# A fused attention and feed-forward kernel: a new order of steps for all five engines

## The chip, the cores and the metric

The kernel runs on one core of one Trainium2 chip. A core has five engines that each take their instructions strictly in turn: TensorE (PE: matrix products, with its weight loads shown apart as PEld), VectorE (DVE), ScalarE (ACT), GpSimd (POOL) and SyncE (SP), which here only starts DMA transfers; ACT and POOL start some as well. The metric is the time of one execution on the device in microseconds; lower is better.

## What is computed

Sparse attention over 4 batches x 8 heads x 768 positions x 64 dimensions, then a feed-forward net (FFN) over the 3072 tokens x 512 features that come out. The reference, cut to what matters:

```python
k_min = np.min(k_chunks, axis=3)            # chunks of 32 keys, 24 per head
k_max = np.max(k_chunks, axis=3)
ub = np.sum(np.maximum(q[:, :, :, None, :] * k_min[:, :, None, :, :],
                       q[:, :, :, None, :] * k_max[:, :, None, :, :]), axis=-1)
ub = np.where(causal, ub, -1000000000.0)
top_chunks = np.argsort(ub, axis=-1)[..., -top_k:]       # the best 6 chunks of each query
scores = scale * np.matmul(q, k.transpose(0, 1, 3, 2))
mask = sel & (pos[:, None] >= pos[None, :])
attn = softmax(np.where(mask, scores, -1000000000.0))
x = np.matmul(attn, v)                      # heads side by side: 3072 x 512
xn = x / np.sqrt(np.mean(x * x, -1) + 1e-06) * rms_g
g = xn @ w_gate                             # 512 x 1536
out = (g / (1.0 + np.exp(-g)) * (xn @ w_val)) @ w_out
```

## The kernel before

The work is cut into twelve blocks of 256 query positions. `ORDER` (L340) lists them as (batch, third of the sequence): block 0 is (0,0), block 4 is (0,1), block 5 is (1,1), block 6 is (0,2), block 8 is (1,2). Each block has two groups of four heads, g = 0 and 1.

**Attention of a block.** k and q arrive by DMA (`load k...`, `load q...`, L376, started by SP, a few by ACT; v by POOL). DVE turns them (`turn k`, `turn q`, L636), takes minimum and maximum of each chunk (`ext0`, `ext1`, L651) and their difference (`dk`, L657). Copies in bf16 (`half k`, `half q`, L643 on ACT or L644 on POOL) feed the scores. For the bounds, q is copied into QX (`qx`, L691/L692) and, from block 4 on, four small transfers per block started by SP bring the other halves across partitions (`qm0` to `qm3`, L706); `relu` (L731 on ACT, L733 on POOL or DVE) needs all four. TensorE makes the bounds (`upper`, L522, or L540 for the first blocks), DVE picks the six best chunks (`ubn`, `top`, `mk`, `mt`, `swap`), TensorE makes the scores (`scores`, L760, with the mask added at L771), ACT the exponentials (`exp`, L810), POOL cuts the triangle (`tri`, L780), TensorE multiplies by v (`values`, L836), and DVE divides (`rden`, `norm`, L851 and L855).

**Between the two.** ACT sums squares (`square`, L872), POOL makes the root (`rms`, L878 and L880), and the tokens are scaled. For blocks 0 to 3 TensorE turns them (`turn`, L916); from block 4 on DVE scales (`scale`, L890) and SP starts two transposing DMAs per block, one for each 128 tokens (`across40` and `across41` for block 4, L896), into the tile xsT.

**FFN of a block.** Twelve slices of the hidden layer, two at a time, named by the first: `wg(4, (0, 1)).2` is the gate product of block 4, both token halves, slices 2 and 3 (L960); `wv` the value product (L960 too); ACT takes tanh (L967) and copies the value product for POOL (`vcopy`, L979); DVE makes `tg` (L971); the product `hh` is made by POOL (L982) or DVE (L975). `project4.0` multiplies the slices 0 to 9 of the first 128 tokens by w_out (L1008), and `project4.0+` the last two; `out` (L1023 on ACT, L1026 on DVE) and `store` (L1030, SP) finish.

**Weights and fillers.** w_gate, w_val and w_out come in thirds, started by POOL (`wg0` and so on) in between its other work. While weights and first blocks are on their way, TensorE multiplies the identity (`keep_busy`, L1075): the warm-up products.

**What sets the order.** All steps (1550) are first registered with `plan.op` as `Op` objects, each with its engine, or with several that could do it, its inputs, and the buffers that it takes. Nothing is emitted then. `Plan.run` (L227) walks a tuple of whole numbers, `STEPS` (L47), and emits one step for each: the number divided by 8 is the step, the rest the engine (0 PE, 1 ACT, 2 DVE, 3 POOL, 4 SP). So 5628 is step 703, `load q1210` (a q load of block (1,2)), on SP. A negative number stands for a run of warm-up products. `SLOTS` (L156) says which buffer of its pool each step takes. The order of the emission is the order on each engine; semaphores for data and for buffers are added by the framework.

```python
        for x in self.STEPS:
            if x < 0:
                n, slot = divmod(-x, 16)
                fill[-1](n // 2, slot, n % 2)
                continue
            seq, e = divmod(x, 8)
            o = self.ops[seq]
            o.alts[self.ENGINES[e]][2]()
```

Of the kernel before, what the change touches and what calls it, by code (L numbers as in the profile page):

```python
# [33 lines left out]
class Plan:  # L34
# [13 lines left out]
        27, 228, 233, 249, 244, 131, 123, 34, 155, 3, 99, 257, 276, 83, 203, 281, 67, 268, 107, 291,  # L48
        75, 115, 412, 425, 299, 433, 420, 538, 139, 466, 380, 396, 473, 482, 490, 404, 545, 42, 498,
        388, 522, 506, 515, 179, 594, 529, 611, 315, -688, 616, 562, 601, 672, 554, 626, 571, 681,  # L50
        50, 578, 457, 786, 587, 634, 323, -178, 792, 642, 689, 57, 848, 650, 802, 699, 810, 9, 818,
        857, 443, 658, 865, 665, 826, 875, 834, -208, 704, 1098, 841, -48, 736, 912, 713, 746, 1107,
        922, 754, 721, 930, 1185, 1042, -146, 880, 307, 961, 1114, 889, 19, 731, 1058, 897, 971,
        -146, 760, 1066, 1049, 770, 1075, 778, 977, 1082, 1091, 1170, 907, -211, 1248, 1192, 1257,
        1660, 451, 1130, 1177, 984, 1628, 1138, 936, 195, 1644, 1202, 1265, 1147, 1684, 1121, 1362,
        1210, 1154, 1163, 946, 1275, 1676, -112, 1368, 954, 1668, 1218, 331, 1001, 994, 1424, 1312,
        1636, 1433, 1226, 8384, 1378, 1652, 1011, 1234, 1441, 1322, 1242, 8344, 1386, 1330, 147,
        1451, 1017, 1394, 1402, 1280, 339, 1410, 8369, 1024, 1418, 1289, 1488, 347, 8336, 1498,
        1297, 1034, 355, 8401, 1506, 1456, 8353, 8480, 8410, 1307, 1537, 8362, 363, 1336, 8497,
        8488, 1346, 1547, 1762, 1473, 8528, 8506, 1465, 1851, 8513, 1354, 1483, 1778, 8545, 8379,  # L60
        8536, 1553, 1706, 1512, 371, 8561, 8392, 1522, 1530, 8523, 1834, 1560, 1577, 8432, 1570,
        8417, 1587, 8554, 8696, 8449, 1722, 8571, 8688, 8458, 8721, 1730, 1593, 8584, 8705, 1802,
        1739, 171, 2001, 1747, 1600, 8714, 1755, 8576, 8609, 1610, 1841, 8731, 1856, 8440, 1713,
        2212, 1866, 8427, 1794, 2228, 8736, 8593, 1874, 2260, 1811, 8465, 1771, 2268, 8602, 8784,
        2276, 1882, 2244, 1890, 8792, 1818, 1827, 1898, 8475, 8801, 1906, 8753, 8832, 8817, 1699,
        8762, 1912, 2220, 8810, 8849, 8619, 2008, 2308, 1921, 2236, 8744, 2018, 2252, 1691, 1937,
        2026, 2034, 8624, 8769, 2042, 8858, 1931, 1785, 2050, 8779, 2284, 2057, 2354, 2324, 8888,
        2292, 3050, 2363, 2300, 2064, 1947, 2370, 8632, 2347, 2316, 2073, 2378, 8656, 2332, 2089,
        2083, 2868, 2426, 2804, 2387, 8913, 2099, 2820, 8641, 2450, 8827, 1952, 2844, 2104, 2442,
        8664, 2828, 8880, 1962, 2410, 8673, 2459, 2395, 2852, 2403, 2114, 1976, 1970, 2417, 2900,  # L70
        2122, 8840, 8897, 2836, 2482, 2884, 8928, 1986, 8906, 8865, 2466, 2475, 2499, 3611, 2507,
        2128, 1994, 8923, 8945, 2138, 2512, 2146, 2153, 2924, 8875, 2161, 2916, 8936, 2860, 2522,
        8954, 3476, 2171, 8976, 2530, 2812, 2538, 2946, 8684, 2177, 3508, 2546, 8961, 2186, 2908,
        2554, 8971, 2962, 2561, 2192, 2892, 2986, 9008, 2433, 2876, 2339, 2201, 3484, 3010, 3524,
        2491, 3034, 3532, 3019, 2970, 3540, 2568, 3003, 3492, 8984, 3066, 2577, 4148, 9136, 8994,
        3083, 2593, 3026, 9040, 2587, 9153, 2603, 3516, 2656, 9162, 9057, 3116, 2979, 3043, 9048,
        2953, 4283, 9066, 3500, 2665, 3058, 9004, 9096, 3075, 9073, 4212, 2675, 9088, 3618, 2681,
        3108, 163, 9083, 9121, 4252, 3634, 9144, 9105, 3092, 3642, 2691, 9240, 3100, 9114, 9169,
        3588, 2608, 9131, 9016, 9265, 2618, 3556, 2626, 2696, 9025, 2632, 2706, 4164, 2714, 2720,
        9179, 4236, 9184, 2730, 2745, 2642, 3572, 2650, 2738, 3131, 9232, 4220, 9201, 3682, 3123,  # L80
        4228, 2753, 9192, 9210, 4180, 211, 9249, 3706, 4244, 2763, 3136, 9217, 9258, 2777, 9227,
        9280, 3146, 2769, 3596, 3625, 9275, 5596, 9288, 3154, 3658, 2993, 3564, 3162, 2784, 3580,
        3675, 9313, 9328, 3548, 3691, 2793, 4196, 3722, 2931, 4260, 4172, 9297, 3170, 4204, 9400,
        9306, 4268, 3178, 9496, 4860, 9323, 9425, 9036, 3738, 3185, 9392, 4156, 3698, 3651, 3755,
        4188, 9336, 4290, 9409, 3603, 3764, 3192, 4330, 9521, 3780, 9488, 3747, 9418, 3201, 3772,
        3715, 4402, 9435, 9440, 9345, 3788, 4306, 3217, 9360, 4876, 3730, 4347, 4417, 4339, 9457,
        4354, 3667, 9505, 9466, 8652, 3211, 3232, 4378, 4452, 2939, 9514, 4884, 9536, 3241, 5532,
        4314, 3227, 4444, 9448, 3803, 9553, 4428, 3249, 3795, 9562, 9544, 4868, 4370, 9473, 3304,
        1620, 9569, 4386, 4322, 3808, 4436, 4394, 3313, 9579, 4916, 3329, 9592, 4908, 3818, 9483,
        4892, 4297, 9368, 4924, 3826, 9617, 3834, 3344, 3323, 4940, 9377, 4980, 3339, 3256, 3353,  # L90
        4972, 3842, 3280, 4900, 9584, 4459, 3290, 3361, 4932, 3266, 3850, 9531, 9632, 3274, 9601,
        3298, 3857, 3368, 9610, 5548, 3392, 3378, 9649, 4956, 9627, 9640, 3386, 3402, 4964, 3417,
        3410, 3864, 5580, 9658, 4275, 3425, 5644, 9680, 5002, 3873, 9356, 4363, 5106, 4948, 3889,
        3435, 5564, 5066, 9665, 9388, 3458, 3904, 4465, 3442, 9675, 9712, 3913, 5018, 3883, 3452,
        5026, 3899, 3921, 5090, 3468, 5042, 3976, 5082, 4472, 5059, 3985, 5628, 5122, 5035, 4411,
        5612, 4001, 9688, 4482, 3995, 9720, 9697, 5139, 4016, 4490, 4498, 5049, 4011, 5148, 3928,
        9729, 5172, 3952, 4025, 3938, 5098, 9792, 5156, 3962, 4506, 4033, 5164, 9840, 3970, 3946,
        9809, 4514, 4040, 9865, 9800, 9818, 4521, 5604, 4050, 5714, 9832, 6308, 6356, 5114, 4592,
        9849, 5620, 5179, 4058, 6332, 4064, 4601, 9826, 5572, 5187, 9928, 4074, 5588, 9858, 5011,
        4089, 5652, 9880, 4082, 187, 5075, 4609, 5636, 5723, 5192, 5540, 4097, 6340, 9953, 6324,  # L100
        4528, 4107, 5202, 9897, 5556, 9920, 4537, 9906, 4114, 9752, 9937, 4130, 4547, 4553, 4124,
        9968, 5730, 9777, 9946, 4563, 4568, 9985, 5786, 9875, 5129, 9976, 5674, 4577, 91, 4140,
        9994, 9888, 5803, 4585, 6426, 4995, 9744, 9914, 6316, 6364, 4616, 10002, 9761, 6348, 5738,
        4640, 6244, 4626, 9770, 6292, 4664, 6260, 6442, 10072, 4673, 5690, 5812, 4634, 10256, 6284,
        4689, 4683, 5210, 5218, 6276, 5747, 10089, 10080, 9740, 10281, 219, 9963, 5820, 4650, 4704,
        10098, 6268, 4658, 4987, 10120, 6980, 4713, 7628, 5226, 10208, 10105, 7020, 5754, 5795,
        10137, 10160, 4721, 9787, 10146, 10168, 6506, 6300, 6252, 5698, 4728, 6521, 7036, 5234,
        10177, 5707, 10008, 5683, 5828, 10193, 5762, 10115, 6540, 5241, 6386, 7644, 10186, 10225,
        7028, 4737, 6402, 10248, 10203, 5836, 6450, 6548, 10128, 4745, 10234, 6371, 7676, 6410,
        10016, 6988, 5771, 10296, 6490, 4699, 9708, 10025, 6916, 10265, 5248, 10154, 7636, 10313,  # L110
        4776, 10274, 6532, 5257, 6466, 6556, 4752, 5273, 5267, 6474, 6996, 10304, 5843, 4762, 6948,
        4770, 5667, 5288, 10322, 6956, 10036, 4786, 10216, 5778, 5659, 5297, 7652, 4794, 10040,
        5851, 4801, 10330, 6419, 4809, 5283, 10242, 7660, 5305, 6483, 7004, 6435, 6498, 7012, 4819,
        5856, 6457, 10291, 5360, 5866, 7692, 10048, 7724, 5369, 4826, 5312, 6932, 5336, 5385, 6940,
        5379, 10336, 6964, 5346, 5322, 10057, 5874, 5395, 5330, 7684, 6569, 5882, 4836, 5400, 6562,
        4842, 6576, 5409, 5354, 4852, 5890, 10368, 5417, 5898, 7732, 6586, 6513, 6924, 7098, 5906,
        10344, 7115, 5424, 7708, 10354, 5448, 7740, 5912, 5434, 5458, 10068, 7058, 10376, 7748,
        5921, 5442, 7067, 10496, 6594, 10364, 6602, 7107, 5937, 7716, 10584, 6395, 6972, 10521,
# [988 lines left out]
```

## Time and profile before

| | us |
|---|---|
| median of the 3 runs shown | 291.81 |
| lowest, highest | 290.79, 293.36 |
| the profiled execution | 289.74 |
| span of its trace | 287.9 |

Costliest groups, from the page (line, engine, tiles, count, busy us, mean ns of one):

| group | busy us | mean ns |
|---|---|---|
| L810 ACT exponentials, x104 | 85.7 | 860 |
| L960 PE gate products, x640 | 72.4 | 262 |
| L960 PE value products, x640 | 71.7 | 262 |
| L1008 PE output products, x272 | 65.7 | 370 |
| L982 POOL hh, x48 | 55.5 | 1165 |
| L971 DVE tg, x72 | 48.3 | 678 |

How the profile is read: it comes from one execution. Busy time is given per engine; the span is cut into 40 slices of 7.2 us, each digit a busy share in tenths. A table of stages gives, for each stretch, its length and then the busy time of PE, PEld, DVE, ACT and POOL, the granted clock of TensorE, the mean number of busy DMA engines' shares summed over the stretch, and GB/s. A row of a timeline gives start, length, engine, line, operation, tiles and count, with idle time ahead of it and what ended that in brackets; rows of SPq and ACTq are DMA issues on those engines' queues. Matmuls are pipelined, so two rows can overlap.

### The profile page before, as it was taken

The numbers are of one execution on the slowest core, as the hardware profiler recorded it, in microseconds if no ns is written. First come the engines' busy times: TensorE is split into PE (matmuls) and PEld (weight loads), VectorE is DVE, ScalarE is ACT, GpSimd is POOL, SyncE is SP. The second block draws the span as 40 slices with busy tenths as digits, with TensorE's granted clock in tenths as the row PEclk, the third lists the DMA queues.
The fourth block names the chain that finished last, engine by engine and source line by source line (L and its number), as shares of the span: only waits on it lengthen the run. The fifth ranks groups of instructions, "written<-read, shape, count | busy, mean of one in ns | idle before, by whom it ended". The sixth has DMA issues, their size and how long they took to land.

```text
span 287.9 us, 11300 instructions
## 1 busy us (share of the span) xinstructions
PE 278.4 (97%) x4642; PEld 209.9 (73%) x4670; DVE 216.8 (75%) x626; ACT 207.5 (72%) x356; POOL 166.9 (58%) x267
## 2 busy tenths in 40 slices
PE   8999899999999999999999999999999999999995
PEld 2559796758777857887764886788678967588763
DVE  3998879798899899799989899987564725274341
ACT  2998787778879988967865696877679766564421
POOL 6789888979888774757682384528125316112420
PEclk9999999999999999999999999999999999999999
DMA  8999999998499594488794514913012500412022
GB/s 179 202 204 217 206 212 146 138 145 164 101 164 165 126 184 79 108 130 154 133 180 86 148 27 95 127 7 75 2 53 61 40 2 1 112 21 56 1 93 89
DMA packets 86387, 31.93 MB, mean 111 GB/s; under 512 B 74816, under 2 KB 81728, under 8 KB 86336
## 3 DMA queue, kind: packets, MB, share of 16 engines
q1 hardware_dynamic: 55616, 22.56, 33.5%
q0 software_dynamic: 29712, 7.87, 27.5%
q10 hardware_dynamic: 1008, 0.79, 1.3%
q8 instruction: 36, 0.59, 0.9%
q14 instruction: 15, 0.12, 0.1%
HBM read 28.58 MB, written 6.29 MB: 121 GB/s over the span
## 4 chain that ended last, share of the span: by engine, by line
PE 78%; DMA 6%; DVE 4%; SPq 4%; issue 2%; ACT 2%; POOL 2%; ACTq 0%; DVEq 0%; POOLq 0%
PE F L960 37%; PE F L1008 20%; PE S L760 7%; PE F L836 6%; DMA wg<-in_moe_w_gate_dram 3%; PE S L771 3%; PE F L522 3%; SPq L706 2%; SPq L376 2%; DMA kraw<-in_k_dram 1%; DMA QX<-qT 1%; DVE kx L651 1%; PE F L540 1%; PE F L1075 1%; DVE kT L636 1%
## 5 line engine op out<-in xcount | busy, mean ns | idle before, releaser
L810 ACT ACTIVATE pt<-S 128x1024 bf16<-128x1024 f32 (+3 forms) x104 | 85.7, 860 | 28.6 <-PE S L771 25.2
L982 POOL TENSOR_TENSOR hh<-tg,vs 128x512 bf16<-128x512 bf16 x48 | 55.5, 1165 | 43.6 <-DVE tg L971 27.2
L960 PE MATMUL F<-xsT,wg 128*128 128x256 bf16 (+1 forms) x640 | 72.4, 262 | 1.2 <-issue 1.1
L960 PE MATMUL F<-xsT,wv 128*128 128x256 bf16 (+1 forms) x640 | 71.7, 262 | 0.2
L1008 PE MATMUL F<-wo,hh 128*128 128x512 bf16 (+1 forms) x272 | 65.7, 370 | 2.1 <-issue 0.9
L971 DVE SCALAR_TENSOR_TENSOR tg<-th,F 128x512 bf16<-128x512 bf16 x72 | 48.3, 678 | 24.9 <-ACT th L967 20.0
L960 PEld LDWEIGHTS <-wg 128*128 128x128 bf16 x640 | 56.0, 98 | 10.1 <-issue 1.6
L960 PEld LDWEIGHTS <-wv 128*128 128x128 bf16 x640 | 56.0, 98 | 8.3 <-issue 0.8
L967 ACT ACTIVATE th<-F 128x512 bf16<-128x512 f32 x72 | 43.0, 605 | 12.5 <-PE F L960 11.6
L780 POOL TENSOR_SCALAR_AFFINE_SELECT pt<-pt 128x512 bf16<-128x512 bf16 x48 | 31.7, 666 | 26.3 <-ACT pt L810 26.2
L1008 PEld LDWEIGHTS <-hh 128*128 128x128 bf16 x300 | 27.5, 98 | 25.8 <-issue 1.2
L979 ACT ACTIVATE vs<-F 128x512 bf16<-128x512 f32 x48 | 28.5, 599 | 9.2 <-PE F L960 6.4
L760 PE MATMUL S<-qb,kb 32*128 32x256 bf16 (+1 forms) x800 | 32.7, 253 | 0.3
L651 DVE TENSOR_REDUCE kx<-kT 128x16 f32<-128x512 f32 x48 | 31.1, 669 | 0.2
L836 PEld LDWEIGHTS <-pt 128*128 128x128 bf16 x672 | 25.4, 98 | 3.7 <-issue 0.2
L836 PE MATMUL F<-VX,pt 128*128 128x65 bf16 x672 | 27.4, 194 | 0.2
L975 DVE TENSOR_TENSOR hh<-tg,F 128x512 bf16<-128x512 bf16 x24 | 16.1, 679 | 10.2 <-PE F L960 10.0
L760 PEld LDWEIGHTS <-kb 32*128 32x128 bf16 x800 | 13.8, 92 | 13.1 <-issue 11.6
L376 POOL DMA_DIRECT2D VX<-in_v_dram x24 | 22.8, 949 | 0.0
L771 PE MATMUL S<-mtd,chunkrow 32*128 32x128 bf16 (+2 forms) x384 | 20.3, 203 | 0.0
L855 DVE TENSOR_TENSOR xnat<-F,rden 128x256 bf16<-128x256 f32 x48 | 19.5, 415 | 0.8
L636 DVE STREAM_TRANSPOSE kT<-kraw 128x512 f32<-128x512 f32 x24 | 16.4, 694 | 4.7 <-DMA kraw<-in_k_dram 4.1
(73 smaller groups left out, 336.8 us busy)
## 6 DMA issues: line engine op xcount, KB each, us to landing
out_dram<-osb SPq DMA_DIRECT2D x23, 256.0 KB, 2.8
kraw<-in_k_dram SPq DMA_DIRECT2D x72, 64.0 KB, 3.3
qraw<-in_q_dram SPq DMA_DIRECT2D x72, 64.0 KB, 2.9
VX<-in_v_dram POOLq DMA_DIRECT2D x24, 128.0 KB, 4.9
QX<-qT SPq DMA_DIRECT2D x32, 64.0 KB, 2.8
wv<-in_moe_w_val_dram POOLq DMA_DIRECT2D x3, 512.0 KB, 9.0
wg<-in_moe_w_gate_dram POOLq DMA_DIRECT2D x3, 512.0 KB, 7.8
wo<-in_moe_w_out_dram POOLq DMA_DIRECT2D x3, 512.0 KB, 13.1
```

The costliest lines, as they stand in the source:

```text
L376: o.inst = issuer[eng].dma_start(out=dst(), in_=src)
L651: plan.op(f"ext{n}{J}", "DVE", 0.585, 0.67, lambda n=n, op=op: VE.tensor_reduce(out=at(kx)[:, g, n], in_=at(kT).rearrange("p h (j c x) -> ...
L760: TE.matmul(s[a // 2][:, a % 2, c0:c0 + q1 - q0], kbt[r, t, ks], qbt[r, t, q0:q1], start=(t == 0), stop=(t == 1 and not mask), skip_group_ ...
L771: TE.matmul(o, chunkrow[r, BLK * kg + P * e:BLK * kg + P * (e + 1)], mv, start=False, stop=(d == 1), skip_group_check=True)
L780: GE.affine_select(out=d, in_=d, compare_op=ALU.is_ge, fill=0.0, base=0, pattern=[[0, 4], [1, P]], channel_multiplier=-1)
L810: lambda pt=pt, hs=hs, c0=c0, c1=c1, x=sc[hp]: SE.activation(out=at(pt)[:, hs, c0:c1], in_=at(x)[:, :, c0:c1], func=ACT.Exp, scale=SCALE), ...
L836: TE.matmul(o[:, a, :], p_[:, a, off:off + P], vt[:, e, 4 * g + a, :], start=(kb_ == 0 and a == 0), stop=(kb_ == nkb - 1 and a == 3), skip ...
L960: TE.matmul(at(p_)[:, n * W:(n + 1) * W], w[:, g, ht * P:(ht + 1) * P], at(xT)[:, g, x0:x0 + W], start=(g == 0), stop=(g == NP - 1), skip_ ...
L967: plan.op(f"tanh{U}.{hp}", "ACT", 0.48, 0.6, lambda th=th, gp=gp: SE.activation(out=at(th), in_=at(gp), func=ACT.Tanh, scale=0.5), pri - 0 ...
L971: VE.scalar_tensor_tensor(out=at(tg), in0=at(th), scalar=1.0, in1=at(gp), op0=ALU.add, op1=ALU.mult), pri - 30, reads=[th, gp], writes=[tg ...
L982: plan.op(f"hh{U}.{hp}", "POOL", 1.11, 1.16, lambda tg=tg, vs=vs, hh=hh: GE.tensor_tensor(out=at(hh), in0=at(tg), in1=at(vs), op=ALU.mult) ...
L1008: TE.matmul(at(op)[:, cs], at(key)[:, o:o + P], wo[:, ht, cs], start=(ht == 0), stop=(ht == NHT - 1), skip_group_check=True)
```

## The change

`STEPS` and `SLOTS` are replaced; nothing else in the file differs. The same 1550 steps are taken.

- TensorE: 315 steps on both sides, 100 of them at another place, by at most six places. The eight runs of warm-up products go from 21, 5, 6, 1, 4, 4, 6, 3 to 21, 4, 1, 3, 4, 2, 6, 2: 43 instead of 50.
- 36 steps change their engine. In the first block: `half k(0,0,0)` from ACT to POOL; `dk(0,0,0)`, two `bd0` (L676) and `relu(0,0,1)` from DVE to POOL; one more `bd0` in block 1; one load from ACT to SP. Later mostly `half`, `qx` and `relu` between ACT, POOL and DVE; at the end `out10.0` and `out10.1` from ACT to DVE.
- ACT: `table`, the tiny exponential at L390 that loads the table (step 1, code 9), stands third on ACT, ahead of two q loads of block 0; before it stood fifteenth.
- POOL: several memsets of the start stand later; the weight loads keep their sequence.
- SP: of 236 steps 181 stand at another place, by up to 34. `load q1210` (5628) goes from behind the transposes of block 4 to ahead of the copies `qm` of block 5, and `load q1220` (5612) to ahead of those transposes (`across40` 3452, `across41` 3468). Five loads of block (3,1) (6244, 6348, 6364, 6316, 6260) go ahead of `across50` and `across51` (4124, 4140). Ahead of `qm1(0,2)` (4436) stand now also `load k2131`, `load k2130`, `load q2100` (4916, 4908, 4924) and 5628; `load k2121` (4884) stands behind it.

The diff, cut to its first lines and to some that hold these codes:

```diff
     STEPS = (
-        27, 228, 233, 249, 244, 131, 123, 34, 155, 3, 99, 257, 276, 83, 203, 281, 67, 268, 107, 291,
...
-        1620, 9569, 4386, 4322, 3808, 4436, 4394, 3313, 9579, 4916, 3329, 9592, 4908, 3818, 9483,
...
-        5026, 3899, 3921, 5090, 3468, 5042, 3976, 5082, 4472, 5059, 3985, 5628, 5122, 5035, 4411,
...
+        27, 228, 233, 249, 244, 115, 50, 67, 34, 131, 3, 99, 9, 257, 276, 123, 268, 107, 281, 291,
...
+        4156, 9336, 4290, 9409, 3192, 5628, 3715, 3755, 9418, 9488, 3201, 4330, 9435, 9521, 9440,
...
+        4297, 4436, 9368, 3826, 9617, 3834, 4892, 3344, 3323, 9377, 4884, 3339, 3256, 4900, 3353,
...
+        3452, 5026, 3921, 5090, 3899, 3468, 5042, 3883, 3976, 5122, 4411, 4472, 3985, 5604, 5082,
...
+        6244, 5179, 5114, 6348, 4592, 9849, 5636, 5723, 4064, 4058, 5540, 5187, 4601, 9826, 5556,
...
     SLOTS = (
-        0, 0, 1, 0, 1, 1, 0, 0, 1, 0, 0, 0, 0, 1, 1, 0, 1, 0, 0, 1, 2, 3, 0, 0, 1, 0, 1, 0, 0, 0, 1,
...
+        0, 0, 1, 1, 0, 1, 0, 0, 1, 0, 0, 0, 1, 0, 1, 0, 1, 0, 1, 0, 0, 0, 1, 2, 3, 1, 0, 0, 0, 0, 0,
...
```

268 rows, old and new, of tables (SLOTS, STEPS) are left out of this document.

## The prediction

> **What bounds the kernel now.** I read the page first (busy times, slices, chain), then the table of stages, then the timelines of the queues around the places where the order changes.
>
> ```profile
> span 287.9 us, 11300 instructions
> ...
> PE 278.4 (97%) x4642; PEld 209.9 (73%) x4670; DVE 216.8 (75%) x626; ACT 207.5 (72%) x356; POOL 166.9 (58%) x267
> ...
> PE   8999899999999999999999999999999999999995
> ...
> PEclk9999999999999999999999999999999999999999
> DMA  8999999998499594488794514913012500412022
> ...
> PE 78%; DMA 6%; DVE 4%; SPq 4%; issue 2%; ACT 2%; POOL 2%; ACTq 0%; DVEq 0%; POOLq 0%
> ```
>
> TensorE is busy 97% of the span and holds 78% of the chain that ended last. It does the same products before and after, bar seven warm-up ones, so only its idle time can go, and a reordering can add idle time without limit. The stages (in each row: length, then each engine's busy time) say where the idle time is:
>
> ```profile
> 0.00:12.00 12.00, 10.47 (x106) 4.65 (x106) 7.01 (x21) 6.64 (x9) 7.60 (x27) 1.00 1.07 185
> 12.00:24.00 12.00, 11.30 (x239) 7.13 (x238) 11.12 (x46) 11.08 (x26) 10.93 (x23) 1.00 1.43 203
> 24.00:36.00 12.00, 10.78 (x241) 10.02 (x239) 10.20 (x23) 9.56 (x20) 10.24 (x15) 1.00 1.21 217
> ...
> 264.00:288.00 24.00, 20.41 (x151) 14.69 (x151) 7.64 (x12) 7.50 (x14) 5.72 (x5) 0.98 0.16 56
> sum 288.00, PE 278.38 PEld 209.88 DVE 216.80 ACT 207.54 POOL 166.92; mean PE 16.38 PEld 12.35 DVE 12.75 ACT 12.21 POOL 9.82
> ```
>
> Idle in all: 288.0 - 278.38 = 9.6 us, of which 1.53 + 0.70 + 1.22 before 36 us and 3.59 in the last stage. The 228 us between hold only 2.6 us. So three places count: the start, the hand-overs in the dense middle, and the end.
>
> **The start (to 36 us).** Here most steps move: the load of the activation table goes ahead of two of ACT's q loads, six small steps go from DVE or ACT to POOL, memsets go behind them, and seven warm-up products go. The weight loads stay in the same sequence.
>
> ```profile
> 30.23 0.32 PEld L960 LDWEIGHTS <-wg 128*128 128x128 bf16 x5 [1.21 <-issue]
> ...
> 33.10 0.90 PEld L960 LDWEIGHTS <-wg 128*128 128x128 bf16 x16 [0.27 <-DMA wg<-in_moe_w_gate_dram]
> ...
> 35.99 0.90 PEld L960 LDWEIGHTS <-wv 128*128 128x128 bf16 x16 [0.21 <-DMA wv<-in_moe_w_val_dram]
> ```
>
> At 33.10 and 35.99 TensorE waits for weights to land, and the DMA row of the page is at eight or nine tenths for its first ten slices (72 us): the weight stream, not the attention of the first block, sets when the dense part begins. Nothing that the change does alters its bytes or its sequence. Attention that is up to 1.21 + 0.27 + 0.21 = 1.7 us late is hidden there; with that cover gone, each us late would be a us lost. The moved table:
>
> ```profile
> 1.74 3.56 ACTq L376 DMA_DIRECT2D qraw<-in_q_dram  x4
> 5.33 1.28 ACT L643 ACT_TABLE_LOAD   x1 [5.33 <-DMA kraw<-in_k_dram]
> ...
> 7.99 0.71 DVE L636 STREAM_TRANSPOSE qT<-qraw 128x512 f32<-128x512 f32 x1
> ```
>
> It costs 1.28 us and sits ahead of the two loads, which then go out at 1.74 + 1.28 = 3.0; DVE wants q only at 7.99, behind four k steps. The six steps given to POOL fit into what it has free in the first stage, 12 - 7.60 = 4.4 us; in the second it has 12 - 10.93 = 1.1. I take 0 for the whole start; the bounds are -1.7 (all three waits go) and +1.1 (POOL's work slips by what it has free in the second stage, and nothing hides it).
>
> **Warm-up products.** They run where TensorE has nothing else to do, so seven fewer save nothing by themselves.
>
> ```profile
> 1.42 7.63 PE L1075 MATMUL F<-ident 128*128 128x512 bf16 x21 [1.42 <-POOL ident masks.py:199]
> ...
> 10.12 1.25 PE L1075 MATMUL F<-ident 128*128 128x512 bf16 x5
> ...
> 12.13 1.47 PE L1075 MATMUL F<-ident 128*128 128x512 bf16 x6
> ```
>
> From five to six they grow by 0.22 us, yet the first 21 took 0.36 us each: an engine that has just started is slow, though the clock column says 1.00. The first 21 stay. The Trainium skill (TensorE: Matmul & The Clock Gate, Part 1: The HAM clock gate) says that an idle window of about 3.4 us halves the matmul clock again. The 21 slow products agree with a slow start; by that rule thinner fillers could mean a second slow spell, which is a rival below.
>
> **The middle: SP's queue.** From 84 us on SP issues without a pause, so a step pulled forward there makes all behind it late. After the change two q loads of block (1,2) (codes 5628, 5612) stand ahead of the two transposes `across4` (L896) that make block 4's FFN input, and five loads stand ahead of `across5`.
>
> ```profile
> 84.03 2.51 SPq L706 DMA_DIRECT2D QX<-qT  x4
> ...
> 93.08 0.59 SPq L706 DMA_DIRECT2D QX<-qT  x1
> 93.72 3.14 SPq L376 DMA_DIRECT2D kraw<-in_k_dram  x3
> 96.97 1.86 SPq L376 DMA_DIRECT2D qraw<-in_q_dram  x4
> ...
> 105.56 2.68 SPq L896 DMA_TRANSPOSE xsT<-xs  x2
> 108.29 1.48 SPq L376 DMA_DIRECT2D qraw<-in_q_dram  x2
> ...
> 121.87 2.54 SPq L896 DMA_TRANSPOSE xsT<-xs  x2
> 124.47 1.67 SPq L376 DMA_DIRECT2D qraw<-in_q_dram  x3
> 126.19 1.44 SPq L376 DMA_DIRECT2D kraw<-in_k_dram  x3
> ```
>
> ```profile
> DMA to landing us min/median/max: 2.4/3.0/4.5
> ```
>
> ```profile
> 100.85 2.33 PE L1008 MATMUL F<-wo,hh 128*128 128x512 bf16 x9
> ...
> 110.61 1.03 PE L960 MATMUL F<-xsT,wg 128*128 128x256 bf16 x8
> ...
> 128.04 1.05 PE L960 MATMUL F<-xsT,wg 128*128 128x256 bf16 x8
> ```
>
> The second transpose starts at 105.56 + 2.68/2 = 106.90 and lands 3.0 later (the median above), at 109.9. Its reader is the first gate product of block 4, at 110.61 with no wait: 0.7 us to spare, and as little as nothing if it landed later. I take 0.35. A load costs 0.47 (1.86/4) to 0.74 (1.48/2); two of them 0.94 to 1.48, say 1.2. TensorE then waits 1.2 - 0.35 = 0.85 us (bounds 0.24 and 1.48). What is queued behind that product is all of TensorE, so it is paid in full.
>
> The five loads ahead of `across5` cost (1.67 + 1.44) x 5/6 = 2.6 us. Its second half lands at 121.87 + 1.27 + 2.6 + 3.0 = 128.7; the reader stands at 128.04, or 128.9 once the first wait has happened. So it is covered by the first wait, and costs 0.7 without it.
>
> A second way leads to the same transposes. The crossing copy `qm1` of block (0,2) (L706, at 93.08) now stands behind three loads more, net. POOL waits for it:
>
> ```profile
> 97.75 0.61 POOL L733 TENSOR_SCALAR qraw<-QX 128x512 f32<-128x512 f32 x1 [1.80 <-DMA kraw<-in_k_dram]
> 98.33 2.26 POOL L982 TENSOR_TENSOR hh<-tg,vs 128x512 bf16<-128x512 bf16 x2
> ...
> 102.35 0.72 POOL L880 TENSOR_TENSOR ri_all<-ri_all,mhalf 128x2 f32<-128x2 f32 x1
> ```
>
> ```profile
> 103.10 2.31 DVE L890 SCALAR_TENSOR_TENSOR xs<-xnat,ri_all,gB 128x512 bf16<-128x512 bf16 x2
> ```
>
> ```profile
> QX<-qT SPq DMA_DIRECT2D x32, 64.0 KB, 2.8
> ```
>
> POOL's relu at 97.75, two hh products, the rms at 102.35 and DVE's scale (103.10 + 2.31 = 105.41) follow each other without a gap into the transpose at 105.56. Three loads are 3 x 0.47 = 1.4 to 3 x 1.05 = 3.1 us (the k loads at 93.72). But this copy took 4.67 us to reach its reader where 2.8 is the median: the DMA engines were behind by 1.9, and an issue that is late only uses that up. So 0 to 3.1, and 3.1 - 1.9 = 1.2 as the middle: no more than SP's own 1.2, and beside it, not on top.
>
> **The other moves** (100 of 315 TensorE steps change places, by at most six; further steps change between ACT, POOL and DVE) swap neighbours that both have their inputs. I take 0, with -1.3 (half of the middle's 2.6 us idle) and +0.5 as bounds.
>
> **The end.** DVE takes two copies that were ACT's, both ahead of the last products.
>
> ```profile
> 283.81 0.71 PE L1008 MATMUL F<-wo,hh 128*128 128x256 bf16 x5
> ...
> 284.55 0.38 ACT L1023 ACTIVATE osb<-F 128x256 f32<-128x256 f32 x1 [0.93 <-PE F L1008]
> ```
>
> TensorE ends last there and its last eight steps keep their order: 0.
>
> **Sum.** 0 + 0 + 0.85 + 0 + 0 = +0.9 us. The profiled execution took 289.74 us (span 287.9 and 1.84 around it), which becomes 290.6; the median of the three runs shown is 291.81, 2.07 above it, and becomes 292.7.
>
> **The rivals.** A: the late queue is hidden, because TensorE reaches block 4 late anyway or the transposes land early; for it stands the 0.7 us spare, against it that SP never pauses. 291.8.
> B, slower: the crossing copy lands the full 3.1 us late. Relu starts at 100.85, the hh products end at 98.33 + 2.26 + 3.1 = 103.7, and `project3.0` (100.85, its ninth product of about 0.23 us at 102.7) waits 1.0. The transposes start at 108.66, the second lands at 113.0, its reader at 111.6 waits 1.4 more. `across5` comes 3.1 + 2.6 late, lands at 131.8, its reader at 130.4 waits another 1.4. In all 3.8: 295.6. It decides from a landing some 1.2 us late on; for it speaks that POOL takes its steps strictly in turn, against it the 1.9 us of backlog.
> C, faster: the weights land with no wait left (1.7) and half of the middle's idle time goes (1.3): 288.8. Against it: the DMA engines are full in the start.
> D: a second slow clock spell after thinner fillers. The first cost 7.63 - 21 x 0.22 = 3.0 us, of which the weight waits hide 1.7: +1.3, 293.1. Against it: no stage of the start idles over 1.6 of 12 us. It is the case that the Trainium skill's clock-gate page (above) would expect if the idle windows grow long enough; nothing of the price is taken from there.
>
> **The numbers.** Forecast 0.42, A 0.22, B 0.17, C 0.16, D 0.03. Over 1% is 2.9 us, about what runs from 290.79 to 293.36 can tell from no change. Faster by it (below 288.9): most of C and a little of the rest, 0.13. Slower (above 294.7): most of B and a tenth of the forecast's spread, 0.20. Within: 0.67. The range reaches from C's near side, 289.3, to B, 295.6; the forecast's own is 291.0 to 294.3 (its wait of 0.24 to 1.48, with 1.0 either way, by which the lowest run shown lies under the median).
>
> **What would show it.** Right: an idle entry of about a us ahead of the gate product near 110.6, ended by a DMA landing, with SP still unbroken; no change ahead of the weight landings near 33 and 36. Wrong: no wait there (A); idle on TensorE ahead of `project3.0` (B); first dense products before 33 us (C); fillers near 0.4 us each after 9 us (D). A wait at some other hand-over would mean that the swaps are not neutral.

## The result, and the profile after

The changed kernel takes 298.26 us (median of 4 runs, 297.74 to 301.11), the kernel before 291.3; the ratio is 1.0297 [1.0247, 1.0346]. One per cent is 2.9 us. The forecast was 292.7 with a range of 289.3 to 295.6, so it gets slower by far more than forecast. Ratios, here and below, are taken from fast executions alone, since some executions fall into a slower state, so a ratio need not be the quotient of the two medians.

First the page of the changed kernel: span, busy times, and the slices (7.4 us each) of TensorE, its clock and the DMA engines.

```profile
span 296.5 us, 11327 instructions
...
PE 280.0 (94%) x4663; PEld 210.3 (71%) x4663; DVE 215.0 (72%) x618; ACT 210.0 (71%) x362; POOL 165.4 (56%) x269
...
PE   8198999999999998996999999999999999999995
...
PEclk9869999999999999999999999999999999999999
DMA  8999999997779677449397733925016001202022
```

TensorE is busy about as long as before. But it stands almost idle in the second slice, its clock is down in the third, and there are new gaps in the sixteenth and the nineteenth. The table of stages (length, busy time of PE, PEld, DVE, ACT and POOL, clock, DMA, GB/s), then TensorE's waits (in all, times, longest):

```profile
0.00:12.00 12.00, 6.90 (x21) 2.60 (x22) 3.11 (x7) 2.58 (x3) 5.69 (x20) 1.00 1.25 170
12.00:24.00 12.00, 9.36 (x177) 5.21 (x177) 7.82 (x27) 7.76 (x18) 8.68 (x17) 0.72 1.04 141
```

```profile
PE S L760 <- ACT qb L643: 6.3, 1, 6.3
PE F L960 <- DMA xsT<-xs: 3.2, 2, 2.3
```

In the first stage, where TensorE was busy 10.47 us before, it is busy 6.90, and the clock of the second falls to 0.72. The two waits name the places: a copy of q on ACT, and the transposes of two blocks. Output products that both timelines show measure how late TensorE is. In the timeline of before, `project0.0` is this row (`project3.0` stands in the prediction, at 100.85):

```profile
45.46 2.32 PE L1008 MATMUL F<-wo,hh 128*128 128x512 bf16 x9
```

In the timeline of after, these are `project0.0`, `project3.0`, and the first gate products of blocks 4 and 5:

```profile
51.86 2.32 PE L1008 MATMUL F<-wo,hh 128*128 128x512 bf16 x10
...
106.52 2.32 PE L1008 MATMUL F<-wo,hh 128*128 128x512 bf16 x10
...
117.24 1.03 PE L960 MATMUL F<-xsT,wg 128*128 128x256 bf16 x8 [0.90 <-DMA xsT<-xs]
...
136.62 1.03 PE L960 MATMUL F<-xsT,wg 128*128 128x256 bf16 x8 [2.26 <-DMA xsT<-xs]
```

TensorE is 51.86 - 45.46 = 6.4 us late after the start, 5.7 at `project3.0`, and 296.5 - 287.9 = 8.6 at the end. In this execution the start loses 6.4, 0.7 is won back, and the two waits (0.90 + 2.26) account for the last 3. In other traces with the same order of SP these two waits come out otherwise (see the middle, below).

**The start.** The chain that ended last, in its first 15 us, shows what TensorE waited for (start, length, what):

```profile
0.80 3.06 DMA kraw<-in_k_dram
3.86 0.02 issue
3.88 6.54 DMA qraw<-in_q_dram
10.42 2.29 issue
12.71 0.72 DVE qT L636
13.43 0.02 issue
13.45 1.09 ACT qb L643
```

The 2.29 us called issue are a wait that the chain does not name: DVE turns q only when the second of ACT's q loads has landed too, at 12.63. The timelines of ACT and of POOL there:

```profile
1.73 1.28 ACT L390 ACT_TABLE_LOAD   x1 [1.73 <-PEq L1091]
3.02 0.20 ACT L390 ACTIVATE mhalf<-eps 1x1 f32<-1x1 f32 x1
3.88 1.83 ACTq L376 DMA_DIRECT2D qraw<-in_q_dram  x3
```

```profile
13.51 0.40 POOL L733 TENSOR_SCALAR qraw<-qT 128x128 f32<-128x128 f32 x1 [5.36 <-DMA kraw<-in_k_dram]
13.87 0.83 POOL L376 DMA_DIRECT2D wv<-in_moe_w_val_dram  x1
```

ACT is done with the table at 3.22, yet the first q load behind it goes at 3.88, when a k load has landed (3.86). The trace's record of that load says why: it waits on the counter of a k load that ACT started at 0.80. Each load of SP and ACT adds to one of eight landing counters, and one that takes a counter again waits until the load before on it has landed. Before, the eight k and q loads of block 0 had the eight counters; now SP's `load q1000` and `load k1000` of block (1,0) have two of them, and ACT's two q loads come ninth and later. They go 2.1 and 2.7 us later (3.88 and 4.92 instead of 1.74 and 2.21), and by the counters they land 4.2 and 5.3 us later (10.42 and 12.63 instead of 6.19 and 7.35), for loads of block (1,0) and of v now go out ahead of them, and the DMA engines are nine tenths busy. The Trainium skill (DMA: Bandwidth & Descriptors, Issuing engines are not separate DMA queues) says that transfers run on the same 16 DMA engines whichever engine starts them; these landings agree. DVE turns q at 12.71 instead of 7.99; POOL's relu of block 0 waits for the turned q (its row names a k load, but DVE's first turn ends at 13.43, just before it), and the first weight load, `wv0`, stands behind that relu: it goes at 13.87 instead of 9.16.

### The profile page after: what moved, and what is told of

Read it like the earlier page. It is cut to its first block, busy times and chain, and to the rows that moved or that the text cites. A ratio compares the mean times of both kernels' runs of the same rounds, so it can differ in the third digit from the quotient of the medians.

```text
span 296.5 us, 11327 instructions
## 1 busy us (share of the span) xinstructions
PE 280.0 (94%) x4663; PEld 210.3 (71%) x4663; DVE 215.0 (72%) x618; ACT 210.0 (71%) x362; POOL 165.4 (56%) x269
## 4 chain that ended last, share of the span: by engine, by line
PE 79%; DMA 10%; DVE 4%; ACT 3%; issue 2%; SPq 2%; DVEq 0%
PE F L960 40%; PE F L1008 18%; PE S L760 7%; PE F L836 6%; DMA kraw<-in_k_dram 5%; DMA xsT<-xs 3%; PE S L771 2%; PE F L522 2%; DMA qraw<-in_q_dram 2%; PE F L540 2%; SPq L376 2%; ACT pt L810 1%; DVE qT L636 1%; DVE kx L651 1%; PE F L1075 1%
## 5 line engine op out<-in xcount | busy, mean ns | idle before, releaser
L982 POOL TENSOR_TENSOR hh<-tg,vs 128x512 bf16<-128x512 bf16 x48 | 54.9, 1152 | 45.5 <-DVE tg L971 27.9
L1008 PE MATMUL F<-wo,hh 128*128 128x512 bf16 (+1 forms) x300 | 68.3, 371 | 0.0
L1008 PEld LDWEIGHTS <-hh 128*128 128x128 bf16 x300 | 28.1, 98 | 25.7 <-issue 0.4
L760 PE MATMUL S<-qb,kb 32*128 32x256 bf16 (+1 forms) x800 | 33.6, 254 | 6.8 <-ACT qb L643 6.3
L771 PE MATMUL S<-mto,chunkrow 32*128 32x128 bf16 (+2 forms) x384 | 20.1, 203 | 0.1
```

The source lines that it names most:

```text
L760: TE.matmul(s[a // 2][:, a % 2, c0:c0 + q1 - q0], kbt[r, t, ks], qbt[r, t, q0:q1], start=(t == 0), stop=(t == 1 and not mask), skip_group_ ...
L771: TE.matmul(o, chunkrow[r, BLK * kg + P * e:BLK * kg + P * (e + 1)], mv, start=False, stop=(d == 1), skip_group_check=True)
L982: plan.op(f"hh{U}.{hp}", "POOL", 1.11, 1.16, lambda tg=tg, vs=vs, hh=hh: GE.tensor_tensor(out=at(hh), in0=at(tg), in1=at(vs), op=ALU.mult) ...
L1008: TE.matmul(at(op)[:, cs], at(key)[:, o:o + P], wo[:, ht, cs], start=(ht == 0), stop=(ht == NHT - 1), skip_group_check=True)
```

## The experiments

Each kernel changes only `STEPS`, and `SLOTS` in step with it. e2, e6 and e11 are variants of the kernel before, the others of the changed kernel. "Before" is the median of the kernel before in the same comparison.

| run | median us | before | ratio, 95% interval |
|---|---|---|---|
| e1 table behind the q loads | 293.12 | 290.79 | 1.0061 [1.0011, 1.0112] |
| e2 kernel before, table first | 293.19 | 290.79 | 1.0111 [1.0080, 1.0143] |
| e3 SP's loads put back | 298.85 | 290.79 | 1.0288 [1.0232, 1.0343] |
| e4 e1 and e3 | 292.11 | 290.79 | 1.0072 [1.0026, 1.0118] |
| e5 fillers through the gap | 295.92 | 290.39 | 1.0200 [1.0158, 1.0242] |
| e6 kernel before, 43 fillers | 291.03 | 290.39 | 1.0020 [0.9979, 1.0061] |
| e7 weights ahead | 295.54 | 290.39 | 1.0193 [1.0147, 1.0240] |
| e8 q loads on SP | 291.87 | 290.39 | 1.0028 [0.9981, 1.0076] |
| e9 all repairs | 291.20 | 290.94 | 1.0029 [0.9998, 1.0060] |
| e10 e4, copies ahead | 291.58 | 290.94 | 1.0020 [0.9985, 1.0055] |
| e11 kernel before, weights ahead | 290.31 | 290.94 | 0.9980 [0.9947, 1.0014] |
| e12 e5 and e7 | 295.21 | 290.94 | 1.0155 [1.0105, 1.0204] |
| e13 e3, copies ahead | 297.01 | 289.91 | 1.0243 [1.0198, 1.0289] |
| e14 new start, old rest | 295.97 | 289.91 | 1.0208 [1.0168, 1.0248] |
| e15 old start, new rest | 291.64 | 289.91 | 1.0052 [1.0016, 1.0088] |

In the kernels of e1 to e4 the tuples take three lines more, so L643 is L646 there, and so on.

### The two late q loads: e1, e2, e8

e1 (ACT's first steps), and e2 in the kernel before:

```diff
 e1
-load k0020, load k0030, table, load q0000, load q0030, load q1030
+load k0020, load k0030, load q0000, load q0030, table, load q1030
 e2
-load k0020, load k0030, load q0000, load q0030, load q1010, load q1030
+load k0020, load k0030, table, load q0000, load q0030, load q1010, load q1030
```

> The changed kernel with one step moved: the table load stands behind ACT's two q loads of block 0, not ahead of them. Theory L (the table load makes these two loads late, and they alone delay the start by 6.4 of the 8.6 us): the last q load of block 0 lands near 7.5 us instead of 12.6, TensorE's idle 6.3 us near 8 us go, and the time falls from 298.3 to about 292. Rival R (the start is late because of the six small steps given to POOL, or because the clock falls to a half after seven warm-up products fewer): the q loads land early but the time stays above 296.

> The kernel before with the one step moved the other way: the table load ahead of ACT's q loads, nothing else. Theory L: q of block 0 lands 4 to 5 us late, and the time rises from 291.3 to about 297. Rival S (the new order of SP's loads, k1000 and q1010 pulled forward, is needed for it): the loads are late by the table's own 1.3 us, of which 0.6 are spare, and the time rises by 0 to 1 us.

```diff
 e8: ACT
-load k0020, load k0030, table, load q0000, load q0030, load q1030
+load k0020, load k0030, table, load q1030
 e8: SP
-load k0000, load k0010, load q0010, load q0020, load q1000, load k1000
+load k0000, load k0010, load q0000, load q0010, load q0020, load q0030, load q1000, load k1000
```

> The changed kernel with the table load where the change put it, but the two q loads of block 0 that stood behind it are started by SP, with the other two, ahead of those of block 1. Theory L (the place of the two loads in the DMA queues is the cost, not the table load as such): q has landed near 8 us, and the time is that of the run with the table behind the loads, 291.5 to 293.1. Rival (the table load or its wait harms ACT in another way): 296 or more.

e1 takes the loss from 3.0% to 0.6, e8 to 0.3, where it can't be told from the kernel before. In e1 one step has moved behind two others; in e8 the table load is where the change put it. So the table load by itself costs nothing that these runs can tell: it costs what it pushes back. DVE's row in e8, then in e2:

```profile
7.84 1.30 DVE L636 STREAM_TRANSPOSE qT<-qraw 128x512 f32<-128x512 f32 x2 [0.17 <-DMA qraw<-in_q_dram]
```

```profile
11.57 0.71 DVE L639 STREAM_TRANSPOSE qT<-qraw 128x512 f32<-128x512 f32 x1 [3.50 <-DMA qraw<-in_q_dram]
```

In e8 q is turned at 7.84. In e2, one moved step in the kernel before, it is turned at 11.57, 3.6 us late and far more than the table's own 1.3: theory L's mechanism, not rival S's. But the time rises by 1.1%, about 3 us: neither the 6 of L nor the 0 to 1 of S. In its trace TensorE is 4.3 us late at `project0.0` and 3.0 at the end: the old order takes part of a late start back, while the lateness grows in the changed kernel's trace. e14 and e15 take this up.

### What the late q costs: e5, e6, e7, e12

The lateness reaches TensorE in three ways: the attention of block 0 itself, the clock, and the weights behind POOL's relu.

```diff
 e5: the runs of fillers
-21, 4, 1, 3, 4, 2, 6, 2
+47, 4, 1, 3, 4, 2, 6, 2
 e6: the runs of fillers in the kernel before
-21, 5, 6, 1, 4, 4, 6, 3
+21, 4, 1, 3, 4, 2, 6, 2
 e7: POOL
-dk(0,0,0), bd0(0,0,0), relu(0,0,0), wv0, bd1(0,0,0), relu(0,0,1)
+dk(0,0,0), bd0(0,0,0), wv0, wg1, relu(0,0,0), bd1(0,0,0), relu(0,0,1)
```

e12 is e5 and e7 together.

> The changed kernel with 47 instead of 21 products in the first run of fillers, so that TensorE is busy until q is there; all else as in the changed kernel. Theory C (part of the loss is the clock: the 6.3 us without work put TensorE at half clock for a window of some 7 us, granted clock 0.98 over the span): the clock rises to 0.993 or more and the time falls by 2.5 to 3.5 us, to about 295. Rival (the late q loads carry the whole loss): 298, unchanged.

> The kernel before with the changed kernel's numbers of warm-up products (21, 4, 1, 3, 4, 2, 6, 2, in its own places), nothing else. If fewer fillers by themselves let the clock fall: clock 0.988 or below in most executions, 294 or more. If they cost nothing, as predicted: 291, within 0.5.

> The changed kernel with the loads of wv0 and wg1 ahead of POOL's relu of block 0, which waits for q; they go out near 8.5 us instead of 13.9 and 16.2. Theory W (the late q is dear because the weight stream stands behind that relu on POOL): the dense products begin 3 to 4 us earlier and the time falls to 294 to 295. Rival V (the attention of block 0 itself sets the start, and the weights would only wait): the weights land early, the time stays within 1 us of 298.3.

> The changed kernel with 47 products in the first run and with wv0 and wg1 ahead of POOL's relu of block 0: the two edits that gained 2.3 and 2.7 us singly. If the clock and the weight stream are two separate parts of what the late q loads cost: 293.2. If they are the same loss seen twice: 295.5.

The clock of TensorE in three stretches, in the changed kernel and then in e5:

```profile
5.95:12.70 6.75, 2.38 (x11) 0.96 (x10) 1.68 (x3) 1.10 (x1) 1.47 (x4) 1.00 1.71 163
12.75:19.50 6.75, 4.91 (x85) 2.82 (x85) 3.38 (x11) 4.00 (x7) 5.94 (x13) 0.50 0.81 114
19.60:24.00 4.40, 4.35 (x93) 2.39 (x92) 4.29 (x16) 3.76 (x11) 2.65 (x5) 1.00 1.41 182
```

```profile
12.75:19.50 6.75, 6.49 (x138) 3.56 (x137) 4.96 (x20) 4.59 (x10) 6.16 (x13) 1.00 0.82 118
```

After 6.3 us without work the changed kernel runs at half clock from 12.75 to 19.5, though it has work again from 14.59. With fillers through the gap the clock stays at 1.00, and the ratio falls from 1.0297 to 1.0200, 2.8 us. The Trainium skill (TensorE: Matmul & The Clock Gate, Part 1: The HAM clock gate) says that the matmul clock halves after an idle window of about 3.4 us and that these windows run freely; this row agrees. e6 shows that seven fillers fewer are not the cause: the gap is. By the ratios e7 is 3.0 us below the changed kernel; POOL's timeline in e7:

```profile
8.14 0.82 POOL L376 DMA_DIRECT2D wv<-in_moe_w_val_dram  x1
8.96 0.75 POOL L376 DMA_DIRECT2D wg<-in_moe_w_gate_dram  x1
```

So the weights go out early (8.14 instead of 13.87). Together (e12) the two edits give 4.1 us by the ratios, not 5.8; the intervals are too wide to say by how much they overlap. Where the gains lie, `project0.0` shows, in e5, e7 and e12 (51.86 in the changed kernel):

```profile
51.03 2.32 PE L1008 MATMUL F<-wo,hh 128*128 128x512 bf16 x10
```

```profile
50.71 2.32 PE L1008 MATMUL F<-wo,hh 128*128 128x512 bf16 x10
```

```profile
50.16 2.32 PE L1008 MATMUL F<-wo,hh 128*128 128x512 bf16 x9
```

By then the edits have won 0.8, 1.2 and 1.7 us. The 3 to 4 us that theory W expected of the weights are not there; the rest of what e7 and e12 gain in these traces comes later, where their waits for transposes are shorter or gone (next section). Where the rest of e5's gain lies its trace can't show: that execution took 300.05 us, with a wait of 3.7 for the transposes of block 5. And with clock and weights both mended TensorE is still 50.16 - 45.46 = 4.7 us late, about as late as q, which DVE turns at 12.55 in e12 instead of 7.99. So the largest part of the late start is the attention of block 0 itself, as rival V of e7 said of the start, though not of the time.

### The middle: e3, e4, e10, e13

```diff
 e3: SP (loads of blocks (1,2) and (3,1) behind the transposes)
-load q1210 ... load q1220, store2.0, across40, across41
+store2.0, across40, across41, load q1210, load q1220
-... load k3120, across50, across51
+... across50, across51, load k3100, load q3111, load q3131, load q3101, load k3120
 e13: SP, beside e3
-across50, across51, load k3100 ... load k3120 ... qm1(1,2) ... qm3(1,2)
+across50, across51, qm1(1,2), qm0(1,2), qm2(1,2), qm3(1,2), load k3100 ... load k3120
```

e4 is e1 and e3; e10 is e1 and e13.

> The changed kernel with SP's queue mended in two places: the two q loads of block (1,2) behind the transposes of block 4, and the five loads of block (3,1) behind those of block 5; the start is left as it is. Theory M (the issue time of these loads is the wait): TensorE's waits for xsT of 0.9 and 2.3 us go, 298.3 becomes 295.3. Rival N (the waits come from full DMA engines after the late start): the waits stay over half, 297 or more.

> Both edits of the two runs on the changed kernel together. If L and M hold and add up: 298.3 - 6.4 - 3.0 = 288.9, below the kernel before at 291.3, since the changed order also won about 0.7 us between 73 and 101 us. If they overlap (the late start makes the middle late, or hides in it): about 292.

> The run with both edits (table load behind the q loads, SP's loads behind the transposes) and one more: the four crossing copies of block (1,2) stand ahead of the five loads of block (3,1) too. Theory Q (SP's queue only handed the wait on: relu of block (1,2), now on ACT, waited 2.4 us for the last of these copies, and a copy of the value product behind it held TensorE for 1.6 us): both waits go, 292.1 becomes 290.5. Rival (ACT's order in the changed kernel is late there by itself): the wait stays, 292.

> The changed kernel with its late start, SP's loads behind the transposes of blocks 4 and 5, and the four crossing copies of block (1,2) ahead of the five loads of block (3,1). Theory Q (with a late start SP's queue costs some 3 us, and the run that moved only the loads handed the wait on to these copies): 298.3 becomes 295 to 296. Rival (the late start carries the whole loss, and waits in the middle move about without changing the end): 298, within 1.

e3 shows no gain, though both waits for xsT are gone. TensorE's waits from 108 to 156 us in e3, then ACT's there:

```profile
PE F L963 <- ACT vs L982: 1.2, 1, 1.2
PE F L839 <- DVE ubn L568: 1.1, 1, 1.1
```

```profile
ACT qraw L734 <- DMA QX<-qT: 2.0, 1, 2.0
```

ACT's row is relu(1,2,0), one of the steps that changed engine: POOL took it before. It waits 2.0 us for the last crossing copy of block (1,2), which stands behind the five loads on SP, as it did before the change; behind the relu on ACT waits a copy of a value product, and for that TensorE. The wait was handed on to the next reader of the same queue. e13 puts these four copies ahead of the loads too, and from 60 to 270 us this is all that TensorE waits for:

```profile
PE F L1008 <- issue: 0.6, 4, 0.2
PE F L836 <- DVE ubn L565: 0.2, 1, 0.2
PE F L960 <- DVE xnat L855: 0.2, 1, 0.2
```

Its time is 1.0243, against 1.0297 unmended: 1.6 us, where theory Q said 2 to 3, and the intervals overlap, so only the waits' going is shown, not the gain. In the traces the stretch from `project3.0` to the end of the span is 187.1 us before, 190.0 in the changed kernel, 189.5 in e3 and 188.0 in e13. With an early start the same edits move too little to be told apart (e1 1.0061, e4 1.0072, e10 1.0020).

The two waits are not fixed costs. e1, e5, e7, e8, e12 and e15 leave SP's order here as the change made it. In their traces the wait ahead of block 4's gate product is 0, 0.3, 0, 0.5, 0.9 and 0 us, against 0.9 in the changed kernel's. Ahead of block 5's it is 2.6 in e1 and 3.7 in e5, and none in the other four. It goes with one landing: the second transpose of block 5 lands 4.3 us after its issue in the changed kernel, 4.5 in e1 and 4.7 in e5, but 2.5 to 3.5 in the four. What delays it was not tried.

### The halves, and the repairs: e14, e15, e9, e11

```diff
 up to wv(0,(0,)).8 on TensorE, all engines
-changed kernel (e14); kernel before (e15)
 from there on
+kernel before (e14); changed kernel (e15)
```

> The changed kernel's order up to wv(0,(0,)).8 on TensorE (near 45 us of its trace, all engines, 43 fillers), the order of before for all the rest. If the start carries the whole loss: 298. If the start costs its 6.4 us at 36 us and the order of before takes some of it back, as in the run with only the table load ahead (1.3 us): 296 to 297, and the rest of the loss is the new order of the middle under a late start.

> The other half: the order of before up to wv(0,(0,)).8, the changed kernel's order for all the rest. If the new order of the middle costs nothing when the start is on time: 290.9, within 0.7 of the kernel before. If it costs the wait that the prediction forecast (0.9) or more: 291.8 to 293.

The new start alone costs 2.08%, 6.0 us; the new rest alone 0.52%, 1.5 us [0.5, 2.6]; both 2.97%, 8.6 us. The 1.1 us more than the sum is within the intervals. In e15's trace TensorE waits for no transpose at all, but ACT's relu(1,2,0) waits for its crossing copy again, with the old start, and TensorE a little for ACT:

```profile
ACT qraw L731 <- DMA QX<-qT: 1.4, 1, 1.4
```

```profile
PE F L960 <- ACT vs L979: 0.4, 1, 0.4
```

e9 is e8 with the middle of e13 and 24 products in the first run:

```diff
-21, 4, 1, 3, 4, 2, 6, 2
+24, 4, 1, 3, 4, 2, 6, 2
```

> The changed kernel with all repairs at once: the two q loads of block 0 on SP, the loads that were pulled ahead of the transposes of blocks 4 and 5 behind them, the four crossing copies of block (1,2) ahead of the five loads of block (3,1), 24 products in the first run of fillers. If the late q loads and SP's queue are all that is wrong with the changed order: 290 or a little less, not slower than the kernel before (290.4 in the last comparison). If some other swap costs as well: 291.5 or more, with a wait on TensorE outside these places.

At 1.0029 [0.9998, 1.0060] the repaired order can't be told from the kernel before: what other swaps cost is at most 0.6%. e11, the kernel before with earlier weights:

```diff
 e11: POOL
-load v001, ones1, bd1(0,0,0), ones6, relu(0,0,0), wv0, dk(0,0,1), bd1(0,0,1), wg1
+load v001, ones1, wv0, wg1, bd1(0,0,0), ones6, relu(0,0,0), dk(0,0,1), bd1(0,0,1)
```

> The kernel before with the loads of wv0 and wg1 some 3.7 us earlier on POOL, ahead of two steps of block 0 that wait for k and q. If the weight stream bounds the start, as the prediction said: TensorE's waits for weights near 33 and 36 us shrink and the time falls by 0.5 to 1.5 us. If the DMA engines are full anyway, the weights only push back q and k of block (1,0): 290.4, or up to 1 us more.

It is the fastest of all, but its interval holds 1. `wv0` went out 3.9 us earlier (5.30 instead of 9.16) and landed 0.2 earlier (15.71 instead of 15.86). With q on time the DMA engines are full then, and the time of this issue matters little. No version that beats both kernels was found.

## Why the prediction was wrong

**The step that failed** is "I take 0 for the whole start", and in it "the two loads, which then go out at 1.74 + 1.28 = 3.0; DVE wants q only at 7.99". It sets the time of an issue against the time of a use and leaves the landing out: the start was priced at 0 and costs 6.0 us (e14). The load issued at 2.21 landed at 7.35: 0.64 us to spare, not 5. And the delay was taken as the table's own 1.28, where ACT's loads also lost their place to loads of SP and POOL; so 2.7 us of issue became 5.3 of landing. e1 and e8 show the place of these two loads to be the cause.

**"The weight stream, not the attention of the first block, sets when the dense part begins"** was read from waits for weights at 33 and 36 us. It failed twice. The weight loads stand on POOL behind a relu that needs q, so a late q makes the stream late (13.87 instead of 9.16). And with the weights early and the clock up, the dense part still begins as late as q is (e12). Nothing of the 1.7 us of cover was seen: in e2 q is turned 3.6 us late, and `project0.0` is 4.3 late.

**Warm-up products at 0**: nothing seen against it (e6, 1.0020 [0.9979, 1.0061]). **Rival D**, a slow spell of the clock after thinner fillers: the spell came, with another trigger (the gap, not the fillers). Against D's 1.3 us, e5 gains 2.8 by the ratios, of which its trace shows 0.8 by `project0.0`.

**The wait ahead of block 4's gate product**: forecast 0.85, seen 0.90 at 117.24, ended by the transposes, in the execution with the late start. The path is the forecast one, but that the size agrees is luck of this execution: in other traces with the same order of SP the wait is 0 to 0.9. **`across5`** was to be covered by that wait. It wasn't: 2.26. The five loads were to make SP 2.6 later; it reached these transposes 129.83 - 121.87 = 8.0 us later than before, when TensorE was 6.6 late, so 1.4. But the first issue took 2.26 instead of 1.23, and the second transpose landed 4.3 us after its issue, 3.2 before: some 2 us that the forecast did not have. These rows are the transposes' issue times in after (least, median, longest, from 129.8 us) and before (from 121.9):

```profile
L896 SPq DMA_TRANSPOSE xsT<-xs x2: 1202/1730/2259, 129.8 to 132.2; - x2
```

```profile
L896 SPq DMA_TRANSPOSE xsT<-xs x2: 1212/1222/1233, 121.9 to 123.2; - x2
```

**The sum for all but the start** was +0.9; e15 measures 1.5 [0.5, 2.6], which does not contradict the size. But the forecast's wait for the transposes is not in e15's trace; the wait seen there is behind relu(1,2,0), whose move to ACT was among the swaps priced at 0. It accounts for 0.4 us on TensorE; where the rest of the 1.5 lies is open. **The crossing copy** `qm1(0,2)` and rival B: no wait ahead of `project3.0` in after. **The end** at 0: nothing seen against it.

## What to carry to other kernels

For a load that is moved, compare its landing, not its issue, with its first use; where the DMA engines are full, what counts is which loads get ahead of it, and that is decided by engines that the edit doesn't touch. Ask of each transfer that seems to set the pace which compute step its issue stands behind, on its own engine. And where a queue is full, putting one group of transfers forward again can merely hand the wait to the next reader: name that reader before measuring.

## What was not expected of the hardware

A short gap can be enough for the slower clock. In e10 and in e4 TensorE stood idle for 2.3 and 2.1 us before block 0's scores, and the stage from 12 to 24 us was granted 0.74 and 0.86 (e10, then e4):

```profile
9.98 0.29 PE L760 MATMUL S<-qb,kb 32*128 32x128 bf16 x8 [2.31 <-ACT qb L643]
```

```profile
12.00:24.00 12.00, 11.51 (x186) 5.83 (x184) 8.59 (x32) 8.65 (x20) 8.74 (x18) 0.74 1.30 217
```

```profile
10.03 0.29 PE L763 MATMUL S<-qb,kb 32*128 32x128 bf16 x8 [2.08 <-ACT qb L646]
```

```profile
12.00:24.00 12.00, 11.39 (x228) 6.36 (x227) 9.54 (x35) 9.59 (x21) 9.73 (x19) 0.86 1.33 212
```

The clock-gate page of the Trainium skill named above gives an idle window of 3.4 us for this; here the gaps were shorter. And single issues on SP took 2.3 us where their neighbours of the same kind took 1.2 (the rows above); what holds them up was not tried.
